# One written order for the first two chunks of an attention and feed-forward kernel, and sign bits put in by ScalarE

## The chip, the cores and the metric

One core of a Trainium2 chip. The metric is the device time of one execution in microseconds (us); lower is better. The engines of the core are TensorE (PE, with its weight loads as PEld), VectorE (DVE), ScalarE (ACT), GpSimd (POOL) and SyncE (SP, which here issues loads).

## The reference

Local attention with global tokens, then a feed-forward layer. Inputs are float32, the two weight matrices float64.

```python
scores = q @ k.T / sqrt(64)                 # 4 batches, 8 heads, 768 rows, head size 64
keep   = (pos_k < n_global) | ((0 <= rel) & (rel < n_local))      # 8 global keys, 96 local ones
dist   = where(global and not local, n_local, abs(rel))
scores = where(keep, scores - 2.0 ** -(head + 1) * dist, -1e9)
a      = exp(scores - max(scores)); a = a / (sum(a) + 1e-9)
x      = (a @ v) as 3072 rows of 512
h      = x @ w_in                                                 # 512 x 2048
out    = (0.5 * h * (1 + erf(h / sqrt(2)))) @ w_out               # 2048 x 512
```

## The kernel before, in words

The 3072 rows are cut into 12 chunks of 256; the 2048 hidden columns into 8 slices of 256. A step (c, s) is chunk c times slice s: a first-layer product into a bank `h` (`m1`, two halves f of 128 columns), Gelu (`gelu`: ScalarE makes `gr`, VectorE its high half `gh` in float16 and the low half `gl`), and a second-layer product into the two halves k of the chunk's output `acc` (`m2`). Each product runs as three float16 products (high x high, high x low, low x high).

Chunks 0 and 1 go through slice after slice together, since the weights are decoded meanwhile; later chunks go through all slices one after the other, with the next chunk's attention between. `STEPS` holds the steps in order: (0,0), three empty places, (0,1), (1,0), (1,1), (0,2), (1,2), (0,3) and so on. From slice 2 on the two chunks share products of 512 columns (L727).

Attention of a chunk goes by pairs of heads: scores into two banks (`scores_pair`), a reduction on VectorE that adds the penalties and finds the largest (L527), exponentials with sums on ScalarE (L561), sums and reciprocals (L570, L573) and scaling (L579) on VectorE, three transposes a head on TensorE (`flip`, L600), copied by ScalarE (L605), products with the values (`av_pair`, L674), and a high half of x by ScalarE (L699, L706) and a low half by VectorE (L211). The scaled probabilities `n` have three buffers.

Weights arrive as float64, four pieces of 512 KB a slice, each as 512 pairs of 32-bit words. A piece is decoded in these parts: the low word is shifted (L249 on GpSimd for slices 0 and 1, L251 on ScalarE for the others); VectorE masks the high word (L257), puts in the sign (L260), joins the low bits (L262); ScalarE makes the high half in float16 (L272) and VectorE the low half (L212 with `winl` or `woutl`). Below, mask, sign and join are the three VectorE parts.

What sets the order: `run` records the work step by step, a scheduler with a timeline of its own puts each engine's instructions in order, and `after` ties single instructions to others. `FILL` and `FILL_T` place products of zeros, `warm_ps`, between the products of the first attention. Each engine then runs its own queue in order, and waits at its head hold up all behind. SyncE's queue issues the loads in order; a load waits when its buffer is taken.

Of the kernel before, what the change touches and what calls it, by code (L numbers as in the profile page):

```python
# [7 lines left out]
F32 = mybir.dt.float32  # L8
# [36 lines left out]
GAP = 3  # L45
STEPS = [(c, s) for s in range(NST) for c in range(2)]
# [40 lines left out]
BLOCKS = (NV - 1, 0, 3, 10, 4, 1, 5, 9, 6, 2, 7, 8)  # L87
WORDS = [T for T in range(33, 90) if T % 2 or T in (62, 70, 78)]
# [26 lines left out]
def slope(h):  # L115
    return 2.0 ** (-(h + 1))


class Fast:
    def __init__(self, tc, ctx, qT, kT, v, w, out, limits):  # L120
# [29 lines left out]
        self.last_unit, self.turns, self.late_rows, self.lows, self.put_off, self.last_max = None, False, [], None, None, None  # L150

    def consts(self):
# [5 lines left out]
        self.scr = const.tile([P, 1], F32, name="scr")  # L158
# [75 lines left out]
    def split_weights(self, s, i):  # L234
        nc = self.nc
        if i == 0:
            if s == LATE:
                self.early.close()
                self.wts = self.ctx.enter_context(self.tc.tile_pool(name="wlate", bufs=1, side="right"))
            if s == NST - 1:  # L240
                self.words.close()
                self.wts = self.ctx.enter_context(self.tc.tile_pool(name="wlast", bufs=1))
            for nm, dst, shape in (("win", self.win, [P, 4, 256]), ("wout", self.wout, [P, 2, 512])):
                dst[s] = tuple(self.wts.tile(shape, F16, name=f"{nm}{k}{s}") for k in "hl")
            self.sw[s] = self.wts.tile([P, 2, 4, 256], F16, name=f"sw{s}")
        w = self.raw.pop((s, i, "w"))
        lw, hw = w[:, :, 0], w[:, :, 1]
        if s < POOLED:
            nc.gpsimd.tensor_scalar(out=lw, in0=lw.bitcast(U32), scalar1=2.0 ** -29, scalar2=None, op0=ALU.mult)  # L249
        else:  # L250
            ins = nc.scalar.activation(out=lw, in_=lw.bitcast(U32), func=AF.Copy, scale=2.0 ** -29).ins  # L251
            if len(self.his) > 1:
                self.after(ins, self.his[-2], "a piece begins when ScalarE is through with the last but one")
            if self.last_table is not None:
                self.after(ins, self.last_table, "a piece comes behind the exponentials of earlier steps")
# [9 lines left out]
    def part_weights(self, s, i):  # L265
        nc = self.nc
        af = self.words_of.pop((s, i)).bitcast(F32)
        if i < 2:
            hi, lo = (x[:, 2 * i:2 * i + 2, :].rearrange("p d f -> p (d f)") for x in self.win[s])
        else:  # L270
            hi, lo = (x[:, i - 2, :] for x in self.wout[s])
# [20 lines left out]
    def load_first(self):  # L292
# [11 lines left out]
        self.raw[0] = (kr, qr)  # L304

# [44 lines left out]
    def load(self, c):  # L350
# [17 lines left out]
        kr = self.nat.tile([P, NP, KW + 96 if cc == 0 else 2 * KW], F32, name=f"kr{c}", tag="kn",  # L368
# [3 lines left out]
        if cc == 0:  # L372
            keys(0, CT, k0)
            keys(CT, 96, k0)
            keys(CT + 96, NG, k0)
# [98 lines left out]
    def scores_pair(self, c, p):  # L474
# [10 lines left out]
        if (c, p) in FILL_S:  # L485
            self.zeros(FILL_S[c, p], sp[0].rearrange("q j k -> q (j k)"))
        prev = self.last_unit if self.turns else self.last_av if EVENTS[c] is not EVF else None
        for j in range(2):
            for a in range(1 if c == 0 and j == 0 else 2):
                for hh in range(2):  # L490
# [3 lines left out]
                    if c == 0 and j == 0:  # L494
                        out, lhs, rhs = sp[hh][:, 0, 0:P], qq[hr, 0:P], kt[hr, 0:P]
                    elif first and j == 0:
                        out, rhs = out[:, 0:P], kt[hr, 0:P]
                    else:
                        if first:
                            rhs = None  # L500
                        elif j == 0:
                            rhs = pairs(kt[hr, :], 96, 96 if a else -96, NC)
                        else:
                            rhs = pairs(kt[hr, :], KW + 192 * a, -96 if a else 96, NC)
                    parts = [(out, rhs)]
                    if c == 0 and j:
                        x = HQ * 3 if a else NG
                        parts = [(out[:, o:o + n], kt[hr, k:k + n]) for o, n, k in ((0, NX, x), (NX, NG, 0), (NX + NG, NC, NC))]
                    for to, keys in parts:
                        ins = nc.tensor.matmul(to, lhsT=lhs, rhs=keys, start=True, stop=True).ins  # L510
                        if prev is not None:
                            self.after(ins, prev, "heads and halves in turn")
                        prev = ins
            if (c, p, j) in FILL:
                prev = self.warm(FILL[c, p, j], prev)
        self.last_unit = prev
        for h in (2 * p, 2 * p + 1) if c == 0 else ():
            ins = nc.vector.tensor_scalar(out=self.pens[:, h, :], in0=self.pen, scalar1=8.0 * slope(h), scalar2=None, op0=ALU.mult).ins
            if self.last_max is not None:
                self.after(ins, self.last_max, "penalties of a pair behind the maxima of the pair ahead")  # L520
# [13 lines left out]

    def zeros(self, n, out):
        prev = self.last_t
        for i in range(n):
            ins = self.nc.tensor.matmul(out, lhsT=self.wz[:, 0:P], rhs=self.wz[:, 0:out.shape[1]],
                                        start=True, stop=True, skip_group_check=True).ins
            self.after(ins, prev, "behind the transposes of the head before")  # L540
            prev = ins
# [51 lines left out]
    def flip(self, c, h):  # L593
# [3 lines left out]
        if (c, h) in FILL_T:  # L597
            self.zeros(FILL_T[c, h], tp.rearrange("k i q -> k (i q)"))
# [8 lines left out]
        if (c, h) == (1, H - 1):  # L607
            scr = nc.scalar.activation(out=self.scr, in_=self.nmax[:, 3 * NP, 0:1], func=AF.Gelu)
            self.after(scr.ins, ins, "behind the last probabilities")
            self.table(scr)  # L610
# [39 lines left out]
    def av_pair(self, c, p):  # L650
# [3 lines left out]
        if p < 2:  # L654
            if c + p == 0:
                self.xs = self.xp.tile([P, 3, NP, 2, CT], F16, name="x")
            self.x[c] = self.xs[:, c % 3]
# [55 lines left out]
    def m1(self, t, f):  # L713
# [16 lines left out]
        prev = self.last_av if (c, s, f) == (0, 1, 1) else self.in_turn if (c, s) in ORDERED and f == 0 else None  # L730
        for d in range(NP):
            for w, e in ((wh, 0), (wh, 1), (wl, 0)):
                ins = nc.tensor.matmul(hp[:, f, :], lhsT=w[:, d, fs], rhs=x[:, d, e, :],  # L733
                                       start=n == 0, stop=n == 3 * NP - 1).ins
                if n == 0 and prev is not None:
                    self.after(ins, prev, "first steps in turn")
                self.turn(ins)
                n += 1
        self.in_turn = ins
# [153 lines left out]
    def m2(self, t, k):  # L893
# [22 lines left out]
        for f in range(2):  # L916
            for g, w in ((gh, wh), (gh, wl), (gl, wh)):
# [3 lines left out]
                if n == 0 and (c, s) in ((0, 1), (1, 0)):  # L921
                    self.after(ins, self.in_turn, "first steps in turn")
                n += 1
        if (c, s) == (0, 1):
            self.in_turn = ins
# [19 lines left out]
    def att(self, T, what, odd=0):  # L945
        for c in range(NCH):
# [37 lines left out]

    def run(self, flag_i):
# [15 lines left out]
        for self.T in range(START[0] - 1, last):  # L1001
# [3 lines left out]
            for (s, i), t in DECODE.items():  # L1005
                if T == t + 1:
                    self.part_weights(s, i)
# [282 lines left out]
```

## Time and profile before

| | |
|---|---|
| median of 3 runs | 610.51 us (610.33 to 613.46) |
| the profiled execution | 609.26 us, of which the span is 607.5 us |
| PE busy | 590.3 us, 97% |
| DVE busy | 480.4 us, 79% |
| ACT busy | 352.1 us, 58% |
| POOL busy | 90.8 us, 15% |

The span goes from the first to the last instruction of the profiled execution. Busy shares are means over stages that have different limits: in the first 60 us TensorE has idle time, later almost none. A matmul's end is modelled, so the row of a matmul can reach into the next one's; the start of the next row tells what a piece costs.

### The profile page before, as it was taken

How to read it: one execution, taken by the hardware profiler on the slowest of the kernel's cores; microseconds unless marked ns; L12 is line 12 of the kernel's file. 1: busy time of each engine (PE TensorE's matmuls, PEld its weight loads, DVE VectorE, ACT ScalarE, POOL GpSimd, SP SyncE). 2: the span in 40 equal slices, each digit the busy share in tenths (PEclk: the TensorE clock that was granted, in tenths of full speed). 3: DMA queues.
4: the chain of work that ended last, by engine and by line, in shares of the span. 5: the costliest groups of instructions: out<-in, count | busy, mean ns of one | idle time of the engine just before them, and what ended most of it. 6: DMA issues, size and time to landing. Idle time of an engine off the chain costs nothing.

```text
span 607.5 us, 18201 instructions
## 1 busy us (share of the span) xinstructions
PE 590.3 (97%) x7377; PEld 456.9 (75%) x7377; DVE 480.4 (79%) x1503; ACT 352.1 (58%) x817; POOL 90.8 (15%) x196
## 2 busy tenths in 40 slices
PE   8889999999999999999999999999999999999996
PEld 6656544445676666888888888888888888888885
DVE  7889999986758964676877877877877877877876
ACT  3577568685647646465566565565565565563332
POOL 3240006222112022021021021021021021020000
PEclk9899999999999999999999999999999999999999
DMA  8948935362521274183194184185284185100001
GB/s 263 254 169 202 335 131 168 100 135 83 138 61 54 89 173 123 38 225 107 55 225 122 40 223 121 67 200 139 83 201 153 64 204 151 66 14 2 36 2 40
DMA packets 105561, 76.74 MB, mean 126 GB/s; under 512 B 53120, under 2 KB 93056, under 8 KB 105472
## 3 DMA queue, kind: packets, MB, share of 16 engines
q1 hardware_dynamic: 102896, 71.85, 42.7%
q10 hardware_dynamic: 2576, 3.67, 1.8%
q8 instruction: 60, 0.98, 0.7%
q14 instruction: 29, 0.24, 0.1%
HBM read 69.21 MB, written 6.29 MB: 124 GB/s over the span
## 4 chain that ended last, share of the span: by engine, by line
PE 81%; DVE 9%; ACT 4%; DMA 3%; issue 1%; POOL 1%; SPq 1%; ACTq 0%; DVEq 0%; POOLq 0%
PE h L733 35%; PE seven L828 24%; PE acc L918 7%; PE av L631 4%; PE s L447 4%; PE acc L903 3%; PE h L727 3%; ACT n L561 2%; DMA w<-w 2%; DVE wb L262 1%; DVE wb L260 1%; DVE n L579 1%; DVE n L527 1%; POOL n L579 1%; SPq L323 1%
## 5 line engine op out<-in xcount | busy, mean ns | idle before, releaser
L733 PE MATMUL h<-x,winh 128*128 128x256 f16 x1344 | 225.2, 273 | 1.1 <-DVE x L211 1.1
L733 PE MATMUL h<-x,winl 128*128 128x256 f16 x672 | 183.1, 273 | 0.0
L733 PEld LDWEIGHTS <-winh 128*128 128x128 f16 x1344 | 130.5, 98 | 21.3 <-issue 1.5
L579 POOL TENSOR_SCALAR n<-n,su 128x160 f32<-128x160 f32 (+1 forms) x160 | 73.0, 474 | 413.6 <-DVE su L573 293.0
L775 ACT ACTIVATE sh<-ss 128x512 f16<-128x512 f32 x64 | 40.3, 630 | 80.5 <-DVE ss L773 80.5
L733 PEld LDWEIGHTS <-winl 128*128 128x128 f16 x672 | 65.7, 98 | 8.2 <-issue 0.7
L768 ACT ACTIVATE gr<-h 128x512 f32<-128x512 f32 x64 | 38.1, 595 | 56.6 <-PE h L733 54.0
L212 DVE SCALAR_TENSOR_TENSOR gl<-gr,gh 128x384 f16<-128x384 f32 (+1 forms) x96 | 57.4, 598 | 10.3 <-ACT gh L889 10.0
L561 ACT ACTIVATE n<-n,mn 128x160 f32<-128x160 f32 x144 | 59.8, 416 | 6.7 <-DVE mn L463 6.0
L773 DVE TENSOR_TENSOR ss<-gr 128x128 f32<-128x128 f32 x128 | 30.9, 281 | 34.6 <-ACT gr L768 34.6
L828 PE MATMUL seven<-sw,sh 128*128 128x256 f16 x384 | 57.4, 273 | 0.0
L828 PEld LDWEIGHTS <-sh 128*128 128x128 f16 x512 | 50.1, 98 | 5.7
L212 DVE SCALAR_TENSOR_TENSOR sl<-ss,sh 128x512 f16<-128x512 f32 x64 | 44.1, 689 | 9.4 <-ACT sh L775 9.2
L828 PEld LDWEIGHTS <-gh 128*128 128x128 f16 x384 | 35.9, 98 | 7.6 <-issue 3.3
L463 DVE CUSTOM_DVE_ANT_0 n<-s,pens 128x160 f32<-128x160 f32 x131 | 35.4, 317 | 5.3 <-PE s L447 5.3
L828 PE MATMUL seven<-sw,sl 128*128 128x256 f16 x192 | 36.6, 273 | 0.1
L774 ACT ACTIVATE gh<-gr 128x384 f16<-128x384 f32 x64 | 33.5, 523 | 2.0
L561 ACT ACT_TABLE_LOAD x22 | 28.2, 1283 | 7.0 <-DMA qr<-qT 6.7
L828 PE MATMUL seven<-wouth,gh 128*128 128x256 f16 x128 | 31.7, 274 | 0.0
L828 PE MATMUL seven<-woutl,gh 128*128 128x256 f16 x128 | 31.5, 273 | 0.0
L211 DVE TENSOR_TENSOR x<-av,x 128x256 f16<-128x256 f32 x41 | 15.3, 414 | 20.5 <-ACT x L644 20.0
L885 ACT ACTIVATE gr<-h 128x512 f32<-128x512 f32 x32 | 19.1, 596 | 20.9 <-PE h L733 16.9
(172 smaller groups left out, 1206.0 us busy)
## 6 DMA issues: line engine op xcount, KB each, us to landing
w<-w SPq DMA_DIRECT2D x32, 512.0 KB, 5.7
c<-w SPq DMA_DIRECT2D x32, 512.0 KB, 4.2
kr<-kT SPq DMA_DIRECT2D x34, 320.0 KB, 4.8
qr<-qT SPq DMA_DIRECT2D x11, 512.0 KB, 4.9
kr<-kT SPq DMA_DIRECT2D x83, 64.0 KB, 4.0
vr<-v SPq DMA_DIRECT2D x24, 176.0 KB, 3.0
out<-o SPq DMA_DIRECT2D x14, 256.0 KB, 2.0
out<-o ACTq DMA_DIRECT2D x8, 256.0 KB, 2.2
```

The costliest lines, as they stand in the source:

```text
L212: return self.nc.vector.scalar_tensor_tensor(out=out, in0=in_, scalar=scale, in1=hi, op0=ALU.mult, op1=ALU.subtract)
L447: ins = nc.tensor.matmul(home[n, u][hh][NG * i:NG * i + NG, :], lhsT=qq[hr, i, o:o + NG], rhs=kt[hr, i, j, k:k + NW], start=not (shared an ...
L463: ins = nc.vector.tensor_tensor_reduce(out=nn[:, 2 * hh + u], in0=home[n, u][hh], in1=pens, scale=-0.125, scalar=3e38, op0=ALU.add, op1=AL ...
L561: self.table(nc.scalar.activation(out=nn, in_=nn, func=AF.Exp, bias=mn[:, i:i + 1], scale=-1.0, accum_out=su[:, i:i + 1]))
L579: ins = eng.tensor_scalar(out=nn, in0=nn, scalar1=su[:, i:i + 1], scalar2=0.0, op0=ALU.mult, op1=ALU.add)
L733: ins = nc.tensor.matmul(hp[:, f, :], lhsT=w[:, d, fs], rhs=x[:, d, e, :], start=n == 0, stop=n == 3 * NP - 1).ins
L768: self.table(nc.scalar.activation(out=gr.rearrange("p i q -> p (i q)"), in_=hp.rearrange("p f q -> p (f q)"), func=AF.Gelu, scale=1.0 / (W ...
L773: self.last_sum = nc.vector.tensor_tensor(out=ss[:, o], in0=x, in1=y, op=op).ins
L774: nc.scalar.activation(out=gh, in_=gr[:, 1:], func=AF.Copy, scale=GS)
L775: self.last_table = nc.scalar.activation(out=sh, in_=ss, func=AF.Copy, scale=GS).ins
L828: ins = nc.tensor.matmul(out, lhsT=g, rhs=w, start=s == 0 and name in ("P1", "P4", "P6", "P3") and i == 0, stop=s >= NST - 4 and i == 2, s ...
L918: ins = nc.tensor.matmul(acc, lhsT=g[:, f, ks], rhs=w[:, f, :], start=s == 0 and n == 0, stop=s == NST - 1 and n == 5).ins
```

## The change

Both chunks' attention, the steps (0,0), (0,1), (1,0), (1,1) and the decoding of slices 0, 1 and 2 no longer go through the loop of `run`. A table, `FRONT`, holds 296 entries, each a letter for a kind of work and figures for chunk, pair or slice and part. `first_steps` records them in the table's order, and `queue` ties each instruction to the last of its engine, so that each engine's order is the table's. Letters that appear below: S scores, R reduction, E exponentials, U sums, N scaling, T transposes, P copy, V values, H and L the halves of x, m and n first and second layer, g Gelu, x and y its halves, w, a, b or s, c, h, l the parts of a weight piece. The loop goes on from step (0,2).

The sign of slice 2's four pieces is put in by ScalarE (`f_sign`, entries s20 to s23) into the upper half of the low word, where the join picks it up; VectorE's sign part stays for slices 0 and 1, and in the loop for later ones.

Chunk 1's keys are loaded once, 352 columns a head pair row, in place of eight loads that laid them out twice; each score product over 192 keys becomes three, over 64, 32 and 96 keys, and the 32 global keys are read from chunk 0's tile. Of the products of zeros, 9 at the start and 6 more stay (`WARM`). A tiny Gelu (`scr`) that loaded Gelu's table early is gone; the first Gelu now comes behind the last exponentials of chunk 1.

```diff
+WARM = {"00": 2, "01": 4}
-FILL = {(0, 0, 1): 4, (0, 1, 1): 9, (0, 2, 1): 4, (0, 3, 1): 4, (1, 0, 1): 4}
-ORDERED = ((1, 0), (1, 1))
-FILL_T = {(1, 6): 6}
-FILL_S = {(1, 1): 0}
+FRONT = ("S00 Q00 W00 R002 R003 E002 R000 R001 E003 Q03 E000 S02 Q02 E001 Q01 U00 N001 S01 N003 N000 R020 w00 N002 "
...
+RESUME = 7
+SCALAR = ()
+SIGNS = ((2, 0), (2, 2), (2, 1), (2, 3))
...
-        kr = self.nat.tile([P, NP, KW + 96 if cc == 0 else 2 * KW], F32, name=f"kr{c}", tag="kn",
+        kr = self.nat.tile([P, NP, CT + NC if c == 1 else 2 * KW], F32, name=f"kr{c}", tag="kn",
                            padded_shape=[P, NP, 4 * KA])
         sync(qr, dap(self.qT, q0, every + [[1, CT]]))
         keys = lambda o, n, k: sync(kr[:, :, o:o + n], dap(self.kT, k, every + [[1, n]]))
-        if cc == 0:
-            keys(0, CT, k0)
-            keys(CT, 96, k0)
-            keys(CT + 96, NG, k0)
+        if c == 1:
+            keys(0, CT + NC, q0 - NC)
...
+    def queue(self, engine, *every):
+        for ins in every:
+            if engine in self.tails:
+                self.after(ins.ins, self.tails[engine], "order of the first steps")
+            self.tails[engine] = ins.ins
+
+    def first_steps(self):
+        for key in FRONT.split():
...
+    def f_scores(self, c, p):
+        kt, qq = (r[:, p] for r in self.raw[c])
+        sp = self.sp[c, p] = [self.bank([P, 2, NK], f"s{c}_{2 * p + hh}") for hh in range(2)]
+        for j in range(2):
+            for a in range(1 if c == 0 and j == 0 else 2):
+                for hh in range(2):
...
+                        x, o = (P + 160 * a, 0) if j else (160 * a, NC + NG)
+                        parts = [(out[:, o:o + NX], kt[hr, x:x + NX]),
+                                 (out[:, NX if j else NC:][:, 0:NG], self.kr0[hr, p, 0:NG]),
+                                 (out[:, NX + NG if j else 0:][:, 0:NC], kt[hr, 192 if j else 64:][:, 0:NC])]
+                    for to, keys in parts:
+                        self.queue("t", self.nc.tensor.matmul(to, lhsT=lhs, rhs=keys, start=True, stop=True))
...
+    def f_sign(self, s, i):
+        w = self.raw[s, i, "w"]
+        hw = w[:, :, 1]
+        if (s, i) in SIGNS:
+            sign = w.rearrange("p f t -> p (f t)").bitcast(F16).rearrange("p (f t) -> p f t", t=4)[:, :, 1]
+            self.queue("a", self.nc.scalar.activation(out=sign, in_=hw, func=AF.Copy, scale=2.0 ** -60))
+        else:
+            a = self.words_of[s, i]
+            self.queue("v", self.nc.vector.scalar_tensor_tensor(out=a, in0=hw, scalar=-0x40000000, in1=a,
+                                                                op0=ALU.bitwise_and, op1=ALU.bitwise_or))
...
-        for self.T in range(START[0] - 1, last):
+        self.xs = self.xp.tile([P, 3, NP, 2, CT], F16, name="x")
+        self.x = {c: self.xs[:, c] for c in range(2)}
+        self.first_steps()
+        for self.T in range(4, last):
```

In the following rows a name like `s1_2` is the tile s of chunk 1, head 2, with a running number behind it; `su0_2` are the sums of pair 2 of chunk 0, and `wb2_3` are the words of piece 3 of slice 2.

SyncE's queue from the queries of chunk 1 to slice 1's words, before:

```order
L323 DMA qr_175<-qT 128x4x256
L323 DMA kr_176<-kT 128x4x160
L323 DMA kr_176<-kT 128x4x64 x2
L323 DMA kr_176<-kT 128x4x160
L323 DMA kr_176<-kT 128x4x32 x4
L323 DMA vr_186<-v 96x512
L323 DMA vr_186<-v 32x512 x2
```

and now:

```order
L330 DMA qr_174<-qT 128x4x256
L330 DMA kr_175<-kT 128x4x352
L330 DMA vr_178<-v 96x512
L330 DMA vr_178<-v 32x512 x2
L330 DMA vr_178<-v 96x512
L330 DMA vr_178<-v 64x2x512 x2
L236 DMA w_0_185<-w 128x1024
```

Eight loads of keys have become one; the values and the words of slice 1 stand behind it as before.

VectorE's queue ahead of the first reduction of chunk 1, before:

```order
L579 TENSOR_SCALAR n0_3_451<-n0_3_451,su0_3_428 128x192
L212 SCALAR_TENSOR_TENSOR winl0_329<-wb0_1_402,winh0_328 128x512
L257 TENSOR_SCALAR wb0_2_469<-w0_2_171 128x512
L260 SCALAR_TENSOR_TENSOR wb0_2_469<-w0_2_171,wb0_2_469 128x512
L527 ISA n1_0_510,nmax_128<-s1_0_496,pens_127 128x192
```

and now:

```order
L1164 ISA wb0_0_352<-w0_0_166,wb0_0_352 128x1024
L1023 TENSOR_SCALAR n0_1_326<-n0_1_326,su0_1_325 128x128
L1023 TENSOR_SCALAR n0_1_326<-n0_1_326,su0_1_325 128x192
L1023 TENSOR_SCALAR n0_2_314<-n0_2_314,su0_2_313 128x128
L1023 TENSOR_SCALAR n0_2_314<-n0_2_314,su0_2_313 128x192
L1148 TENSOR_SCALAR wb0_2_464<-w0_2_170 128x512
L1023 TENSOR_SCALAR n0_2_314<-n0_2_314,su0_2_313 128x192
L1008 ISA n1_0_478,nmax_128<-s1_1_427,pens_127 128x192
```

The reduction now comes ahead of the sums and scalings of chunk 0's last pair, and of most of the decoding of slice 0's pieces 0, 1 and 2.

VectorE's queue around the low half of step (1,1) (`gl6`), before:

```order
L212 SCALAR_TENSOR_TENSOR woutl2_776<-wb2_2_843,wouth2_775 128x512
L257 TENSOR_SCALAR wb3_0_893<-w3_0_209 128x512
L212 SCALAR_TENSOR_TENSOR woutl2_776<-wb2_3_848,wouth2_775 128x512
L257 TENSOR_SCALAR wb3_1_898<-w3_1_211 128x512
L887 TENSOR_SCALAR gh6_984<-gr6_986 128x512
L260 SCALAR_TENSOR_TENSOR wb3_0_893<-w3_0_209,wb3_0_893 128x512
L257 TENSOR_SCALAR wb3_2_950<-w3_2_213 128x512
L260 SCALAR_TENSOR_TENSOR wb3_1_898<-w3_1_211,wb3_1_898 128x512
L212 SCALAR_TENSOR_TENSOR gl6_985<-gr6_986,gh6_984 128x512
```

and now:

```order
L226 SCALAR_TENSOR_TENSOR woutl2_879<-wb2_3_952,wouth2_878 128x512
L1109 TENSOR_SCALAR gh6_993<-gr6_991 128x512
L226 SCALAR_TENSOR_TENSOR woutl2_879<-wb2_2_966,wouth2_878 128x512
L226 SCALAR_TENSOR_TENSOR gl6_994<-gr6_991,gh6_993 128x512
L266 TENSOR_SCALAR wb3_0_1023<-w3_0_201 128x512
L266 TENSOR_SCALAR wb3_1_1028<-w3_1_203 128x512
L266 TENSOR_SCALAR wb3_2_1037<-w3_2_205 128x512
```

Five parts of slice 3's pieces that stood ahead of `gl6` stand behind it now.

## Rows read from the trace of the kernel before

**Rows 1.** Busy time by stretch; then granted clock (1.00 is full), DMA share, GB/s:

```profile
10.00:20.00 10.00, 7.63 (x70) 5.80 (x69) 8.72 (x39) 5.18 (x21) 6.99 (x4) 1.00 1.09 309
...
40.00:50.00 10.00, 8.30 (x94) 5.13 (x92) 8.57 (x30) 8.72 (x27) 0.00 (x0) 1.00 0.22 75
50.00:60.00 10.00, 9.50 (x104) 6.91 (x104) 10.00 (x23) 8.20 (x16) 0.00 (x0) 1.00 1.01 233
...
70.00:80.00 10.00, 10.00 (x48) 4.56 (x47) 10.00 (x20) 5.65 (x10) 0.00 (x0) 1.00 0.87 332
```

**Rows 2.** TensorE's timeline, 60 to 66 us: start, duration, instructions:

```profile
60.91 0.39 PE L918 MATMUL acc<-wouth,gl 128*128 128x512 f16 x1 [0.97 <-DVE gl L212]
...
63.08 0.38 PE L733 MATMUL h<-x,winh 128*128 128x256 f16 x2
...
65.70 0.38 PE L918 MATMUL acc<-wouth,gh 128*128 128x512 f16 x1
```

**Rows 3.** VectorE's timeline, 66 to 70 us:

```profile
66.26 0.42 DVE L257 TENSOR_SCALAR wb<-w 128x512 int32<-128x512 int32 x1
...
67.87 0.68 DVE L260 SCALAR_TENSOR_TENSOR wb<-w,wb 128x512 int32<-128x512 int32 x1
68.47 0.41 DVE L257 TENSOR_SCALAR wb<-w 128x512 int32<-128x512 int32 x1
68.81 0.68 DVE L260 SCALAR_TENSOR_TENSOR wb<-w,wb 128x512 int32<-128x512 int32 x1
69.41 0.68 DVE L212 SCALAR_TENSOR_TENSOR gl<-gr,gh 128x512 f16<-128x512 f32 x1
```

**Rows 4.** VectorE's waits to 75 us; then its groups, 28.5 to 70.1:

```profile
DVE su L570 <- ACT n L561: 5.3, 6, 1.4
...
L570 DVE TENSOR_SCALAR su<-su 128x4 f32<-128x4 f32 x4 | 1.1, 275 | 2.3 <-ACT n L561 2.3
```

**Rows 5.** ScalarE's groups, 20 to 75 us:

```profile
L251 ACT ACTIVATE w<-w 128x512 int32<-128x512 uint32 x10 | 6.2, 671 | 0.0
```

**Rows 6.** VectorE's timeline at the first reductions of chunk 1:

```profile
28.56 0.35 DVE L527 CUSTOM_DVE_ANT_0 n<-s,pens 128x192 f32<-128x192 f32 x1
...
28.83 0.35 DVE L527 CUSTOM_DVE_ANT_0 n<-s,pens 128x192 f32<-128x192 f32 x1
```

**Rows 7.** SyncE's timeline; then loads issued 8:10 and 10:10.6, with landing:

```profile
8.76 0.43 SPq L323 DMA_DIRECT2D qr<-qT  x1
10.37 10.33 SPq L323 DMA_DIRECT2D kr<-kT  x8
...
qr<-qT SPq DMA_DIRECT2D x1, 512.0 KB, 8.7
...
kr<-kT SPq DMA_DIRECT2D x1, 320.0 KB, 8.1
```

**Rows 8.** TensorE's timeline: scores and transposes, two records a float32 product:

```profile
8.51 1.54 PE L510 MATMUL s<-kr,qr 64*128 64x128 f32 x28 [0.46 <-DMA kr<-kT]
...
17.74 0.82 PE L600 MATMUL t<-ident,n 128*128 128x128 f32 x6
...
27.11 0.97 PE L510 MATMUL s<-kr,qr 64*64 64x192 f32 x16
```

**Rows 9.** Busy time by stretch, with the granted clock behind POOL's:

```profile
18.60:20.20 1.60, 0.00 (x0) 0.00 (x0) 1.29 (x7) 1.60 (x7) 0.00 (x0) 1.00 1.11 221
22.20:25.50 3.30, 3.30 (x24) 2.41 (x21) 2.21 (x11) 1.94 (x10) 0.00 (x0) 0.50 0.64 184
```

**Rows 10.** VectorE's timeline, beside GpSimd and without; then GpSimd's group to 75 us:

```profile
32.27 1.51 DVE L579 TENSOR_SCALAR n<-n,su 128x192 f32<-128x192 f32 x4
...
34.04 1.13 DVE L212 SCALAR_TENSOR_TENSOR woutl<-wb,wouth 128x512 f16<-128x512 f32 x1
...
39.12 1.01 DVE L579 TENSOR_SCALAR n<-n,su 128x192 f32<-128x192 f32 x4
...
L249 POOL TENSOR_SCALAR w<-w 128x512 int32<-128x512 uint32 x8 | 13.9, 1733 | 20.9 <-DMA w<-w 20.2 <-DVE n L579 0.4
```

More of the change, by code (lines that the diff above doesn't have):

```diff
@@ L242, in split_weights @@
                 self.wts = self.ctx.enter_context(self.tc.tile_pool(name="wlast", bufs=1))
-            for nm, dst, shape in (("win", self.win, [P, 4, 256]), ("wout", self.wout, [P, 2, 512])):
-                dst[s] = tuple(self.wts.tile(shape, F16, name=f"{nm}{k}{s}") for k in "hl")
-            self.sw[s] = self.wts.tile([P, 2, 4, 256], F16, name=f"sw{s}")
+            self.new_weights(s)
         w = self.raw.pop((s, i, "w"))
         lw, hw = w[:, :, 0], w[:, :, 1]
[L248 to L255, printed above, removed]
+        ins = nc.scalar.activation(out=lw, in_=lw.bitcast(U32), func=AF.Copy, scale=2.0 ** -29).ins
+        if len(self.his) > 1:
+            self.after(ins, self.his[-2], "a piece begins when ScalarE is through with the last but one")
+        if self.last_table is not None:
+            self.after(ins, self.last_table, "a piece comes behind the exponentials of earlier steps")
         a = self.sm.tile([P, 512], I32, name=f"wb{s}_{i}", tag="o", bufs=3)
@@ L267, in part_weights @@
         af = self.words_of.pop((s, i)).bitcast(F32)
[L268 to L271, printed above, removed]
+        hi, lo = self.halves(s, i)
         ins = nc.scalar.activation(out=hi, in_=af, func=AF.Copy, scale=WS).ins
@@ L493, in scores_pair @@
                     out, lhs = sp[hh][a * HQ:(a + 1) * HQ, j, :], qq[hr, o:o + HQ]
[L494 to L497, printed above, removed]
-                    else:
[L499 to L515, printed above, removed]
+                    if j == 0:
+                        keys = pairs(kt[hr, :], 96, 96 if a else -96, NC)
+                    else:
+                        keys = pairs(kt[hr, :], KW + 192 * a, -96 if a else 96, NC)
+                    ins = nc.tensor.matmul(out, lhsT=lhs, rhs=keys, start=True, stop=True).ins
+                    if prev is not None:
+                        self.after(ins, prev, "heads and halves in turn")
+                    prev = ins
         self.last_unit = prev
[L517 to L520, printed above, removed]
         ns = self.pp.tile([P, 2, 2 * NK], F32, name=f"n{c}_{p}", tag="n")
@@ L533, in scores_pair @@
             self.pt_n[c, 2 * p + hh] = nn
[L535 to L541, printed above, removed]
     def warm(self, n, prev=None):
@@ L606, in flip @@
         self.pt_t[c, h] = pt
[L607 to L610, printed above, removed]
     def av_windows(self, c, part):
@@ L945, in att @@
     def att(self, T, what, odd=0):
-        for c in range(NCH):
+        for c in range(2, NCH):
             r = T - START[c]
@@ L1036, in run @@
                 self.gelu(T + 1)
+            if T < RESUME:
+                continue
             self.att(T, "pt", 1)
```

203 lines of the change are left out of this document (180 added, 23 removed), and 13 rows, old and new, of the table FRONT.

## The prediction

> **What bounds the kernel now.** I read the table of stretches first, then VectorE's timeline, TensorE's, the waits, and last the loads. From 70 us on TensorE is busy 10.0 of 10 us in nearly every stretch, and what it does there is the same work in nearly the same order in both programs; so the change is worth what it takes off the front, the part up to the last second-layer product of the first four steps. In the front TensorE waits (7.63 and 8.30 of 10 us, filler products included), while VectorE goes from 8.7 of 10 to 10.0 by 50 us [rows 1]. VectorE sets the pace: at 60.91 TensorE has its last long wait of the front, 0.97 us for a low half that VectorE makes [rows 2].
>
> Where does the front end? VectorE ends its last piece of it, the low half of step (1,1), at 70.01 (start 69.41, and such pieces follow each other every 0.60). Between 66.26 and there stand five pieces that belong to slice 3, not to the front; from start to next start the three masks take 0.34 each and the two sign pieces 0.60, 2.21 in all (one of each mask shown) [rows 3]. So VectorE's front is worth 67.8 us. TensorE has, from 60.91 on and without a pause, 34 products of 512 columns (10 of them last from 60.91 to 63.08, so 0.217 each) and 24 of 256 (63.08 to 65.70, 2.62) [rows 2]: 60.91 + 7.37 + 2.62 = 70.9. It ends 3.1 us behind VectorE.
>
> **What the change does to that.** In the new table VectorE's last piece is again the low half of (1,1). TensorE starts its last 36 second-layer products when the low half of (0,1) is there, 4.3 us of VectorE's table earlier (six pieces of 0.60, two of 0.335); it can pass only four of them before the last words of slice 1 come 0.6 later, so 32 x 0.217 = 6.9 stand behind that, 7.5 - 4.3 = 3.2 us after VectorE. The lag is the old one. What VectorE's table gains, the kernel gains.
>
> Removed from VectorE: four sign pieces. One lasts 0.68, but back to back they cost 0.60 each [rows 3], so 2.4 us. ScalarE gets them; none of its rows is this form, and the nearest is its own piece on the words, 671 ns [rows 5]; it is busy 8 to 9 of 10 us between 40 and 60 and less around them [rows 1], and the early Gelu with its two table loads leaves it, so four times 0.6 cost nothing there. If ScalarE were late, high halves of slice 2 would be, and their price is at most those 2.4 us back.
>
> Removed too: VectorE's waits for exponentials, 5.3 us in six [rows 4]. The first, until the sums at 9.73, is given by the first four exponentials and mostly stays; scaled penalties of two more pairs fill 0.8 of it. The others go if the table always has something else ready.
>
> Added: one wait that I can place. VectorE's first reduction of chunk 1 (28.56 now [rows 6]) stands in the table much earlier. Summing VectorE's new order from the first sums at 9.73, which stay (twelve reductions of 0.25, 3.0, since half of them are narrower than the 0.27 of [rows 6]; three pairs of sums with their reciprocals, an estimated 1.3 from the 0.275 of a sum [rows 4]; twelve scalings of 0.24, 2.9 [rows 10]; three masks, one sign, one join of words, 2.2 [rows 3]; an estimated 1.7 for what GpSimd's pieces stretch meanwhile, from [rows 10]), it gets there at about 20.8. The scores are not there. The keys of chunk 1 are one load of 704 KB instead of eight, behind the queries, which land 8.7 us after 8.76; the first 320 KB of keys land 8.1 after 10.37, 1.0 us later [rows 7]. So 704 KB take 2.2 and land at 19.6; I take 19.5. Then TensorE does the scores of pair 1, transposes of pair 1 of chunk 0, the scores of pair 0, and transposes again (VectorE writes into a buffer that these still read). What 24 products of a pair cost no row shows: 8 products with as many columns take 0.97, and 14 products that are mostly of these pieces 1.54, so by count 2.6 [rows 8]. I take 1.8, nearer the second, because its groups overlap the next by their drain. With transposes at 0.40 a head [rows 8] the reduction can start at 19.5 + 1.8 + 0.35 + 1.8 + 0.45 = 23.9; the ends are 22.2 and 25.5.
>
> The clock makes this later. TensorE idles in the table from about 14.7 to 19.5. Before, an idle stretch from 18.6 to 20.2 was followed by the lower level (1.2 GHz) from 22.2 to 25.5, and then by the full one [rows 9]. At half speed for 3.4 us it loses at most 1.7; I take 0.8, half: 24.7.
>
> From there VectorE's work is what it did before from 28.56 to 70.01, 41.45, less slice 3 (2.21), less its idle time of 2.26 (the two waits of 0.87 and 1.39; [rows 4] has 2.3), that is 36.98; less the signs, 2.4; plus what the old order had done by 28.56 and the new has not: five word pieces of 0.60 (3.0), two low halves of x (0.67), one sums pair and four scalings (1.36), 5.0. Together 39.6. Idle time in it: between 0 and the old 2.26; the table puts several pieces between the last exponential and its sum, so I take 0.6. End: 24.7 + 39.6 + 0.6 = 64.9 against 67.8, a gain of 2.9 us.
>
> Behind the front nothing is added: slice 3's words need 6.1 us of VectorE (four masks, eight pieces of 0.60), the next two steps of TensorE 3.2 + 5.2. POOL's four pieces of slice 1 come earlier, at about 26 to 33 instead of 29.75 to 37.2, since the loads ahead are shorter; there four scalings took 1.51 against 1.01 later without POOL, and a low half 1.13 against 0.68 [rows 10]. The same number of pieces meets the same kind of work; I change nothing.
>
> The Trainium skill (SBUF — State Buffer, section Who interferes with whom) says of that meeting that VectorE and GpSimd take a shared port pair for a whole instruction and the other is blocked until it ends. The rows agree in direction: what is stretched are scalings and pieces with two operands in SBUF. They do not agree in size: a piece of POOL's lasts 1.73 us, and four scalings together lose 0.5 [rows 10]. By the page's rule in full this would be a rival of its own, below.
>
> **Sum.** The profiled execution took 609.26 us (607.5 of span); the median of the runs is 610.51, 1.25 more. 609.26 - 2.9 = 606.4, and on the scale of the median 607.6. A measurement of this kernel can tell about 0.5%, 3.05 us, from no change: the forecast lies at that edge.
>
> **Rivals.**
> - The gain is given back in waits along VectorE's table. For: every engine is now tied in order, and VectorE waits for a low half of x behind product, copy and cast of two other engines; the 0.6 may be 3. Against: before it had the same chains and only 2.3. Time: 606.4 + 2.4 = 608.8, on the median's scale 610.
> - The table runs as if without the wait: scores at 0.97 a pair, no low clock. Then the reduction starts at 22.2, with no idle time the end is 61.8, a gain of 6.0: 604.5. For: the columns are those of the old products. Against: short products repeat a fixed share in the 14-product row.
> - Slower, by TensorE's clock: filler products fall from 40 in all to 15, and in the first 40 us TensorE's work waits in short pieces. If the lower level lasts 15 us after 19.5 instead of 3.4, TensorE loses 7.5 where 0.8 is counted, and VectorE waits for scores and values: +6.7 - 2.9 = 3.8, 614.3. It decides from some 13.5 us of low clock on (2.9 + 3.05 + 0.8 = 6.75 at half a microsecond each). For: the one low stretch of before came with fillers in place. Against: it lasted 3.4 us although TensorE did only small products in it [rows 9].
> - Slower, by GpSimd blocking VectorE: four pieces of slice 1 that hold VectorE up by a whole 1.7 each, 6.8 where the rows have about 0.9: 5.9 - 2.9 = 3.0, 613.5. The traces speak against it, with losses of 0.1 to 0.5 per piece [rows 10]; it is what the page's rule would give.
>
> That the change doesn't do what it says I leave out: each engine's order stands in the built program.
>
> **Chances.** Forecast 0.52, with a range of its own from 605.3 to 609.5; gain given back 0.21; no wait 0.15; clock 0.09; GpSimd 0.03. About half of the forecast's case lies below 607.46 (610.51 - 3.05): faster 0.27 + 0.15 = 0.42; same 0.25 + 0.21 = 0.46; slower 0.12. For the range I go from 603.8, below the no-wait case, to 611.6, above the given-back case; the slower cases lie outside.
>
> **What would show it.** First reduction of chunk 1 at 24.7 (22.2 to 26), with TensorE's scores as what ended VectorE's wait of about 4 us; the keys' landing at 19.5; a low clock of some 3.4 us around 19 to 23; VectorE's last piece of step (1,1) at 64.9; from there on TensorE 10 of 10. Wrong if VectorE idles more than 2 us after its first reduction of chunk 1, if the front ends at 61 or before, or if time goes away or comes behind 75 us.

## The result and the profile after

The changed kernel takes 616.35 us in the median of 7 runs (615.89 to 618.47), the kernel before 610.33 us in 7 runs beside it: a ratio of 1.010, with a 95% interval from 1.0076 to 1.0123. It is slower by 6.0 us where 2.9 us less were forecast, and it lies outside the range. The profiled execution took 615.89 us (span 614.1), 6.6 more than that of before.

The table of stretches of the changed kernel, to be set against [rows 1] (same columns: busy time of TensorE, its weight loads, VectorE, ScalarE, GpSimd, then granted clock, DMA share, GB/s):

```profile
10.00:20.00 10.00, 5.16 (x73) 3.84 (x68) 9.55 (x45) 5.86 (x24) 6.56 (x4) 0.91 1.06 326
20.00:30.00 10.00, 8.47 (x112) 7.06 (x114) 1.43 (x9) 2.42 (x8) 3.07 (x2) 0.50 0.94 280
...
50.00:60.00 10.00, 9.09 (x98) 6.01 (x97) 9.69 (x23) 7.10 (x12) 0.00 (x0) 1.00 0.47 165
60.00:70.00 10.00, 6.07 (x29) 2.90 (x28) 8.82 (x17) 7.08 (x12) 0.00 (x0) 0.83 1.11 307
70.00:80.00 10.00, 10.00 (x48) 4.50 (x47) 9.78 (x19) 4.56 (x9) 0.00 (x0) 1.00 1.04 314
```

One row stands out: from 20 to 30 us VectorE, which sets the pace of the front, is busy 1.43 of 10 us, and TensorE has half its clock. VectorE's timeline shows one wait there:

```profile
20.08 0.31 DVE L1023 TENSOR_SCALAR n<-n,su 128x192 f32<-128x192 f32 x1
28.97 0.36 DVE L1008 CUSTOM_DVE_ANT_0 n<-s,pens 128x192 f32<-128x192 f32 x1 [8.57 <-PE t L1029]
```

The first reduction of chunk 1 starts at 28.97; it stood at 28.56 before [rows 6], with much more done ahead of it. What it waits for is on TensorE (scores, transposes, scores, transposes; the last row is a pair's scores at full clock):

```profile
14.42 1.17 PE L988 MATMUL warm_ps<-wz 128*128 128x512 f32 x4
21.53 2.89 PE L984 MATMUL s<-kr,qr 64*64 64x64 f32 x48 [5.95 <-DMA kr<-kT]
24.35 0.90 PE L1029 MATMUL t<-ident,n 128*128 128x128 f32 x3
25.18 2.92 PE L984 MATMUL s<-kr,qr 64*64 64x64 f32 x48
28.03 0.90 PE L1029 MATMUL t<-ident,n 128*128 128x128 f32 x3
...
33.92 1.76 PE L984 MATMUL s<-kr,qr 64*64 64x64 f32 x48
```

TensorE waits 5.95 us for the keys, and then every piece takes longer than the same piece does at 33.92. The next rows show the clock there: busy time by stretch, with the granted clock behind GpSimd's, to be set against [rows 9]:

```profile
15.60:18.20 2.60, 0.00 (x0) 0.00 (x0) 2.46 (x13) 1.89 (x8) 2.14 (x2) 1.00 1.07 352
18.20:21.50 3.30, 0.00 (x0) 0.00 (x1) 2.19 (x8) 0.00 (x0) 0.00 (x0) 0.51 1.10 251
21.50:31.90 10.40, 10.37 (x124) 8.61 (x124) 2.63 (x12) 3.66 (x12) 4.81 (x4) 0.50 0.74 237
31.90:34.00 2.10, 2.06 (x35) 1.50 (x35) 1.91 (x8) 1.86 (x7) 1.44 (x1) 1.00 0.01 4
```

TensorE does nothing from 15.6 on, the clock falls to the lower level (1.2 GHz) at 18.2, and it stays there to 31.9, through 10.4 us in which TensorE is busy with small float32 products. In the kernel before it came back after 3.4 us.

Later VectorE ends its last piece of the front, and TensorE pauses once more (VectorE's and TensorE's timelines, to be set against [rows 3] and [rows 2]):

```profile
70.10 0.43 DVE L1109 TENSOR_SCALAR gh<-gr 128x512 f16<-128x512 f32 x1 [0.90 <-PE acc L1123]
70.45 0.69 DVE L226 SCALAR_TENSOR_TENSOR woutl<-wb,wouth 128x512 f16<-128x512 f32 x1
71.05 0.68 DVE L226 SCALAR_TENSOR_TENSOR gl<-gr,gh 128x512 f16<-128x512 f32 x1
```

```profile
64.86 0.39 PE L1123 MATMUL acc<-wouth,gh 128*128 128x512 f16 x1 [3.00 <-DVE gh L1109]
...
66.39 0.61 PE L1123 MATMUL acc<-wouth,gl 128*128 128x512 f16 x1 [0.93 <-DVE gl L226]
...
77.38 0.38 PE L1123 MATMUL acc<-wouth,gl 128*128 128x512 f16 x1
```

VectorE's front ends at 71.65 (start 71.05 and 0.60), against 67.8 before. TensorE's ends at 77.60, and from 72.64 on 2.37 us of it are shared products of step (0,2): 75.2, against 70.9 before. So the front is 4.3 us longer. From some 165 us on each Gelu stands 6.1 us later than in the kernel before: another 1.8 come behind the front.

### The profile page after: what moved, and what is told of

The parts are those of the page before. It is cut to its first block, busy times and chain, and to the rows that moved or that the text cites. A ratio compares the mean times of both kernels' runs of the same rounds, so it can differ in the third digit from the quotient of the medians.

```text
span 614.1 us, 18375 instructions
## 1 busy us (share of the span) xinstructions
PE 590.7 (96%) x7480; PEld 457.5 (74%) x7480; DVE 478.4 (78%) x1499; ACT 354.7 (58%) x818; POOL 87.0 (14%) x196
## 4 chain that ended last, share of the span: by engine, by line
PE 80%; DVE 10%; ACT 4%; DMA 4%; issue 1%; SPq 0%; ACTq 0%; DVEq 0%
PE h L701 33%; PE seven L793 24%; PE acc L883 7%; PE av L602 4%; PE s L452 4%; PE h L696 2%; DMA w<-w 2%; DMA kr<-kT 2%; PE acc L868 2%; PE acc L1123 1%; ACT n L538 1%; PE s L984 1%; DVE gl L226 1%; DVE winl L226 1%; DVE wb L269 1%
## 5 line engine op out<-in xcount | busy, mean ns | idle before, releaser
L701 PE MATMUL h<-x,winh 128*128 128x256 f16 x1280 | 214.2, 273 | 0.8 <-DVE x L225 0.8
L701 PE MATMUL h<-x,winl 128*128 128x256 f16 x640 | 174.4, 273 | 0.0
L701 PEld LDWEIGHTS <-winh 128*128 128x128 f16 x1280 | 124.6, 98 | 19.6 <-issue 0.8
L556 POOL TENSOR_SCALAR n<-n,su 128x160 f32<-128x160 f32 (+1 forms) x160 | 70.2, 459 | 425.4 <-DVE su L550 288.5
L733 ACT ACTIVATE gr<-h 128x512 f32<-128x512 f32 x64 | 38.1, 596 | 56.3 <-PE h L701 53.9
L701 PEld LDWEIGHTS <-winl 128*128 128x128 f16 x640 | 62.6, 98 | 7.3
L602 PE MATMUL av<-ptb,vr 32*64 32x128 f32 (+4 forms) x1392 | 30.2, 265 | 0.1
L602 PEld LDWEIGHTS av<-ptb,vr 32*64 32x64 f32 x1392 | 26.0, 131 | 5.4 <-issue 4.2
```

The lines of the kernel that those rows point to most:

```text
L556: ins = eng.tensor_scalar(out=nn, in0=nn, scalar1=su[:, i:i + 1], scalar2=0.0, op0=ALU.mult, op1=ALU.add)
L602: ins = nc.tensor.matmul(banks[i][hh * D:(hh + 1) * D, u0 * NG:u1 * NG], lhsT=vv[rows, b, hh * D:(hh + 1) * D], rhs=g, start=n == 0 and no ...
L733: self.table(nc.scalar.activation(out=gr.rearrange("p i q -> p (i q)"), in_=hp.rearrange("p f q -> p (f q)"), func=AF.Gelu, scale=1.0 / (W ...
```

## The experiments

Each is run beside the kernel before (median 610.0 to 610.9 in the four sets). Where an edit adds a line, a line number in a profile row is one or more higher than in the changed kernel.

**The clock alone: `e1_warm`.** Products of zeros fill TensorE's pause ahead of chunk 1's scores.

```diff
-WARM = {"00": 2, "01": 4}
+WARM = {"00": 2, "01": 32}
```

> The changed kernel with 32 products of zeros instead of 4 between the transposes of head 3 and the first scores of chunk 1, so that TensorE is busy from 14.4 to about 21.4 us, when the keys land. Theory A (the clock: TensorE's pause from 15.6 to 21.5 lets the granted clock fall to 0.5 from 18.3 to 31.6, and scores of 2.9 us a pair and transposes of 0.9 us at that level make the first reduction of chunk 1 late): no low stretch, scores 1.8 a pair and transposes 0.45, the first reduction at 25.9 to 26.2 instead of 28.97, and the execution 3 us or more shorter, 613 or less on the scale of the median of 616.35. Theory B (the wait for the keys itself, the clock is only seen beside it): the first reduction no earlier than 28.3, 615.5 to 617.

Measured: 615.94 us (4 runs, 615.18 to 617.78), not to be told from the changed kernel. Yet scores take 1.78 and 1.80 us a pair and transposes 0.55, and the first reduction starts at 26.91, though the keys landed at 22.27 in this execution, 0.9 later. Each theory holds in one half only: the clock does delay the reduction, and the gain is lost again. The stretches around the second pause show where some of it may go:

```profile
55.00:63.80 8.80, 4.98 (x34) 3.03 (x32) 8.32 (x17) 6.68 (x10) 0.00 (x0) 1.00 1.03 307
63.80:70.60 6.80, 5.87 (x15) 2.09 (x15) 5.45 (x11) 2.85 (x5) 0.00 (x0) 0.50 1.08 292
70.60:75.00 4.40, 4.40 (x21) 1.96 (x20) 4.30 (x9) 0.99 (x2) 0.00 (x0) 1.00 1.04 219
```

TensorE is busy 4.98 of 8.8 us ahead of 63.8, and then its products at the end of the front run at the lower level for 6.8 us, where the changed kernel has 3.4. This execution is the slowest of the four (617.78) and has one more low stretch, from 125 to 128.6 us. The run `e10_warm_end` below fills the second pause as well.

**The keys alone: `e2_keys`.** Queries and keys of chunk 1 go ahead of two pieces of slice 0's words.

```diff
-        for i in range(4):
+        for i in range(2):
             self.load_weights(0, i)
         self.load(1)
+        self.after(self.last_load, self.last_word, "keys behind two pieces of words")
+        self.last_word = self.last_load
+        for i in range(2, 4):
+            self.load_weights(0, i)
         self.load_v(1)
```

> The changed kernel with the queries and keys of chunk 1 loaded ahead of the third and fourth piece of slice 0's words. The keys land two pieces of 512 KB earlier, 2.6 us (a piece per 1.3), at about 18.8 instead of 21.4. Theory B (lateness of the keys): the first reduction at about 26.4, the execution 2.5 us shorter, 613.8. Theory A (clock): TensorE still pauses for 3 us from 15.6, the clock still falls at about 18.3, the scores still take 2.9 a pair; the first reduction comes 2.6 earlier as well, but the low stretch stays as long as the work in it is short, 10 us or more, and the execution gains at most 2.5. The two together differ in the next run.

Measured: 613.10 us (10 runs, 610.70 to 615.08). The keys land at 17.57, 3.8 earlier; in the profiled run TensorE pauses 2.09 and the clock does not fall there. The first reduction starts at 22.21, 6.8 earlier, and the Gelu of step (1,1) 5.5 earlier. The ten runs spread over 4.4 us, in line with their mean clock: those at 0.995 or 0.996 took 610.7 to 610.8, those at 0.979 to 0.983 took 613.5 to 615.1. So with the shorter pause the clock is lost in some runs and not in others; at which place the slow ones lost it is not shown, since the profiled run is one of the fast ones.

**Both: `e3_both`.** The edit of `e2_keys`, and 20 products of zeros.

> Both: queries and keys of chunk 1 ahead of two pieces of words, and 20 products of zeros instead of 4 behind the transposes of head 3 (14.4 to 18.8 us). Theories A and B add up: first reduction at 23.3 to 23.7, near the 23.9 that the prediction had without its clock loss; the execution 5.5 us shorter than the changed kernel's, 610 to 611, about the time of the kernel before. If the time then stays above 613, the loss is elsewhere: in VectorE's table behind the first reduction or in the signs on ScalarE.

Measured: 613.99 us (7 runs), where 610 to 611 was expected. The expected reduction time holds (23.52), but this is 1.3 later than in the run before, since the zeros last to 18.98 while the keys are there at 17.49. Fillers that outlast the wait they fill cost time themselves. The second pause is not filled here (granted clock 0.50 from 62.3 to 65.6 us); what the rest of the miss is was not separated.

**The second pause alone: `e6_end`.** The changed kernel with 13 products of zeros ahead of step (0,1)'s second-layer product.

```diff
-WARM = {"00": 2, "01": 4}
+WARM = {"00": 2, "01": 4, "11": 13}
... (from here on parts of lines of FRONT)
-l13 a22 c22 n010 h22
+l13 a22 c22 W11 n010 h22
...
+            out = self.acc[0, 0] if c else self.warm_ps
...
```

> The changed kernel with 13 products of zeros (added into chunk 0's output bank, so nothing is computed otherwise) ahead of the second-layer product of step (0,1), where TensorE pauses from 61.9 to 64.9 us for a high half that VectorE makes, and 0.9 more for the low half; from 66.0 the clock is then at 0.5 for 3.4 us, while TensorE starts on the front's last products. Theory D (this second pause and the low stretch behind it cost time that nothing hides): no low stretch at 66, the later steps 1 to 1.7 us earlier, 614.7 to 615.3 where the changed kernel has 616.35. Theory E (VectorE sets the end of the front, TensorE's clock there is hidden): the later steps at the same times within 0.5, 616 to 616.7.

Measured: 617.31 us (5 runs). The clock stays at 1.00 from 32.6 us on, and steps from 145 us on start within 0.04 us of the changed kernel's: theory E (the medians, 1.0 apart, lie within the spread of these five runs). The stretch from 66 us in the changed kernel and in `e6_end`, and VectorE's last piece of the front in `e6_end`:

```profile
66.00:69.40 3.40, 3.01 (x8) 1.08 (x9) 3.17 (x6) 1.76 (x4) 0.00 (x0) 0.50 1.10 287
66.00:69.40 3.40, 2.95 (x13) 1.28 (x14) 3.37 (x7) 1.76 (x4) 0.00 (x0) 1.00 1.14 294
...
70.18 0.68 DVE L226 SCALAR_TENSOR_TENSOR gl<-gr,gh 128x512 f16<-128x512 f32 x1
```

In the changed kernel this second low stretch (3.4 us, from 66.0) costs time at the end of the front and none at the end: without it VectorE's last piece starts 0.9 earlier (70.18 against 71.05, the wait of 0.90 at 70.10 is gone), TensorE's front, counted as above, ends at 74.0 instead of 75.2, and between 75 and 130 us TensorE waits 2.5 us for VectorE's halves instead of 0.8.

**Both pauses, late keys: `e10_warm_end`.** 32 and 13 products of zeros.

> The changed kernel with late keys as they are, but with both pauses of TensorE filled (32 products of zeros ahead of chunk 1's scores, 13 at the end of the front). The second kernel with filled pauses and early keys took 610.3. If the clock behind the first pause is the larger part of the loss: the first reduction 4.6 us behind the keys' landing and not 7.6, no stretch at the lower level before 600 us, the execution near 613. If lateness of the keys is the larger part: 615 or more.

Measured: 613.65 us (7 runs, 612.82 to 614.07), 2.7 less than the changed kernel. The profiled execution has no low stretch before 600 us. The keys land at 21.87, the first reduction starts 4.64 later; in the changed kernel it is 7.58 (28.97 - 21.39). So the lower clock costs 2.9 us at this place, and 2.5 (Gelus from 165 us on) to 2.7 (medians) of them reach the end. The stretch of the scores, and TensorE's and VectorE's timelines:

```profile
22.20:27.00 4.80, 4.80 (x112) 4.05 (x110) 0.49 (x3) 1.88 (x6) 0.00 (x0) 1.00 1.04 303
```

```profile
22.00 1.77 PE L984 MATMUL s<-kr,qr 64*64 64x64 f32 x48
23.71 0.55 PE L1030 MATMUL t<-ident,n 128*128 128x128 f32 x3
24.19 1.81 PE L984 MATMUL s<-kr,qr 64*64 64x64 f32 x48
25.92 0.55 PE L1030 MATMUL t<-ident,n 128*128 128x128 f32 x3
```

```profile
26.51 0.36 DVE L1009 CUSTOM_DVE_ANT_0 n<-s,pens 128x192 f32<-128x192 f32 x1 [5.82 <-PE t L1030]
```

**Both pauses, early keys: `e7_keys_end`.** 12 and 13 products of zeros, and the edit of `e2_keys`.

> The early keys of the second run (two pieces of words behind them), 12 products of zeros instead of 4 ahead of chunk 1's scores (to about 17.2, just short of the keys' landing at 17.5) and the 13 at the end of the front. Each run of the second kernel lay between 610.7 and 615.1, with a mean clock from 0.996 down to 0.979. Theory D: with both pauses filled the mean clock is 0.999 in most runs, the runs lie closer together, and the median falls from 613.1 to 609 to 611, the time of the kernel before. Theory E: 612.5 to 613.5, and the spread stays.

Measured: 610.33 us (11 runs, 609.76 to 610.86; mean clock 0.998 to 1.000), against 610.32 of the kernel before: the same. Theory D holds here, with a spread of 1.1 us instead of 4.4. Against the run before this one, keys that land 4.3 us earlier (17.56 against 21.87) are worth 3.3 us.

**The order behind the front: `e11_order`.** The last kernel, and ScalarE's cast of slice 0's weight sums is tied behind chunk 2's first Gelu and its high half.

```diff
-        nc.scalar.copy(hi, t)
+        self.cast = nc.scalar.copy(hi, t).ins
...
                 self.gelu(T + 1)
+                if T == 18:
+                    self.after(self.cast, self.last_table, "behind chunk 2's first gelu")
```

> The kernel with early keys and both pauses filled (610.3), and one cast of ScalarE (sums of slice 0's second-layer weights, which waits 3 us for VectorE at 147 to 150 us) placed behind chunk 2's first Gelu and its high half. Theory F (behind the front the old scheduler's order holds up TensorE where it did not in the kernel before: 1.05 us at 153.6 for a high half of ScalarE, whose Gelu stands behind that cast and an output copy): TensorE does not wait there, steps from 155 us on are 1.0 us earlier, 609.3. Otherwise the wait moves to the next place that needs VectorE, and it stays 610.3.

Measured: 608.66 us (12 runs, 607.87 to 609.44), ratio to the kernel before 0.9974, interval 0.9958 to 0.9991: a quarter of a per cent less than the kernel before, and 1.7 us less than `e7_keys_end`. Theory F holds. TensorE in the kernel with early keys and filled pauses, at the place (it is the changed kernel's wait at 159.06, of 1.06):

```profile
152.04 0.38 PE L701 MATMUL h<-x,winh 128*128 128x256 f16 x2
152.25 0.27 PE L701 MATMUL h<-x,winl 128*128 128x256 f16 x1
153.58 0.39 PE L883 MATMUL acc<-wouth,gh 128*128 128x512 f16 x1 [1.05 <-ACT gh L854]
```

and with the cast behind the Gelu:

```profile
151.47 0.38 PE L701 MATMUL h<-x,winh 128*128 128x256 f16 x2
151.68 0.27 PE L701 MATMUL h<-x,winl 128*128 128x256 f16 x1
151.79 0.38 PE L883 MATMUL acc<-wouth,gh 128*128 128x512 f16 x1
```

The wait is gone, and the steps behind are 2.1 us earlier in the profiled runs, 1.7 in the medians, more than the 1.05 expected: 0.6 of it is already there at 152, ahead of the edit, from a shorter wait for x at an earlier step.

**The signs back on VectorE: `e5_signs`** (the changed kernel) **and `e13_signs_back`** (the kernel of `e11_order`).

```diff
-SIGNS = ((2, 0), (2, 2), (2, 1), (2, 3))
+SIGNS = ()
...
... (parts of lines of FRONT)
-U12 h10 N120 s20 N121 l10
+U12 h10 N120 N121 l10
...
-V13 a20 y00
+V13 a20 s20 y00
```

The entries s21, s22 and s23 move in the same way, each behind its a.

> The changed kernel with slice 2's four signs back on VectorE, each right behind its mask. If moving them was worth the 2.4 us of the prediction: 618.7. Theory C (ScalarE's sign takes 1.1 us a piece and not 0.6, sits between copies and Gelu, and holds up the joins, so that nothing was gained): 616.4, no change, or shorter.

> The best kernel so far (early keys, both pauses filled, ScalarE's cast behind chunk 2's first Gelu: 608.7) with slice 2's four signs back on VectorE, each behind its mask; the clock is at full level here, so it doesn't blur the term as it did in the run with the changed kernel's late keys (620.5 against 616.4). The prediction's term: four pieces of 0.60 on VectorE that the front's end follows one for one, 611.1, and the Gelu of step (1,1) 2.4 us later. If it is much less (under 609.5), VectorE did not set the front's end. If more (612 or above), the old scheduler's order behind the front has changed with it, and the 2.4 is read from the Gelu of step (1,1).

Measured: 620.54 us (4 runs), 4.2 more than the changed kernel, and 609.99 us (11 runs), 1.3 more than `e11_order`, where 2.4 more was expected. The second is read without a change of clock. There the Gelu of step (1,1), on ScalarE's timeline of `e11_order` and of `e13_signs_back`:

```profile
63.02 0.58 ACT L1100 ACTIVATE gr<-h 128x512 f32<-128x512 f32 x1
```

```profile
65.75 0.58 ACT L1100 ACTIVATE gr<-h 128x512 f32<-128x512 f32 x1
```

2.73 later: the term of 2.4 is about right at the front's end, while 1.7 are left behind 140 us; behind the front the loop's order differs between the two programs. Theory C falls, although ScalarE's piece is even longer than it says (group of the changed kernel, 20 to 75 us; two in a row took 2.50 in `e8_before_sign`):

```profile
L1156 ACT ACTIVATE w<-w 128x512 f16<-128x512 int32 x4 | 5.4, 1350 | 0.1
```

**The signs alone, without the table: `e8_before_sign` and `e9_before_signs`**, the kernel before with its old scheduler; `SIGNS` is (2,) in the first and (2, 3, 4) in the second.

```diff
...
-        nc.vector.scalar_tensor_tensor(out=a, in0=hw, scalar=-0x40000000, in1=a,
-                                       op0=ALU.bitwise_and, op1=ALU.bitwise_or)
+        if s in SIGNS:
+            sign = w.rearrange("p f t -> p (f t)").bitcast(F16).rearrange("p (f t) -> p f t", t=4)[:, :, 1]
+            self.after(nc.scalar.activation(out=sign, in_=hw, func=AF.Copy, scale=2.0 ** -60).ins, ins_w, "sign behind the shift")
+        else:
+            nc.vector.scalar_tensor_tensor(out=a, in0=hw, scalar=-0x40000000, in1=a,
+                                           op0=ALU.bitwise_and, op1=ALU.bitwise_or)
```

> The kernel before with slice 2's four signs on ScalarE, each behind its shift, everything else by the old scheduler. If VectorE sets the front's end there too: 2.4 us of VectorE go and 607.5 to 609 is left of 610.4. The other way: ScalarE's sign lasts 1.1 us net and stands ahead of Gelu and high halves in its queue, the joins wait for it, and the time is 610.4 or more.

> The same with the signs of slices 2, 3 and 4 on ScalarE. VectorE is busy 10.0 of 10 us up to 90 us in the kernel before, so 4.8 us more go from it there; but TensorE has only 0.9 us of pause between 60 and 90. If the front alone counts: as the run before, within 0.5 us. If TensorE's pauses of 2 us between 90 and 130 come from VectorE's backlog: 1 to 2 us shorter than the run before.

Measured: 618.46 us (5 runs) and 617.06 us (5 runs), against 610.32. Slower by 8.1 and 6.7, and the second 1.4 less than the first. The waits of the first from 20 to 150 us (engine and line, releaser: us in total, times, longest):

```profile
DVE gh L893 <- ACT gr L891: 4.7, 3, 3.4
DVE gh L893 <- PE acc L909: 3.6, 1, 3.6
...
PE h L733 <- ACT gr L891: 3.6, 1, 3.6
```

VectorE and TensorE now wait for Gelu. The old scheduler places all four engines' work anew once one piece moves, so these runs tell what this edit does to that program, not what four pieces on ScalarE cost by themselves: whether the pieces' length or the new order makes Gelu late was not separated. The profiled run of the first also has two low stretches of TensorE's clock, around 22 to 29 and 134 to 138 us.

**Later signs: `e12_late`.** The kernel of `e7_keys_end`, with slices 3 and 4 signed by ScalarE in the loop (the edit just shown, for those slices).

> The kernel with early keys and both pauses filled (610.3), and the signs of slices 3 and 4 on ScalarE too, in the loop behind the table. VectorE is busy 9 to 10 of 10 us from 60 to 130 us; 8 pieces of 0.6 us go from it, and TensorE's waits for VectorE between 88 and 130 (2.6 us: 1.3 for a low half, 1.1 for x, 0.2 for a high half) can fall by that: 608 to 609.5. Other way: ScalarE's 8 more pieces of 1.1 us stand ahead of Gelu as they did in the kernel before with signs on ScalarE (617 to 618), and it takes 611 or more.

Measured: 613.17 us (10 runs), 2.8 more than `e7_keys_end`: the second of the two outcomes. TensorE again waits for Gelu (2.5 us at one place), with the same limit on what this shows.

```profile
PE h L701 <- ACT gr L855: 2.5, 1, 2.5
```

## Why the prediction was wrong

Term by term, in the profiled executions: the first reduction of chunk 1 starts at 28.97 where 24.7 was forecast, 4.3 later (1.9 from the keys, 2.1 from the clock, 0.2 from scores and transposes); from there to VectorE's last piece of the front it takes 42.7 in place of 40.2, 2.5 more; TensorE ends 3.6 behind VectorE in place of 3.1; and 1.8 come behind the front, where nothing was forecast. Together that is 9 us, the distance from 2.9 less to 6.1 more.

The experiments take the time back in other portions, in medians: the changed kernel 616.35; the clock kept up 613.65 (2.7 less); early keys 610.33 (3.3); the order behind the front 608.66 (1.7). These 7.7 us are not the forecast's errors one by one: the first takes away all that the low clock cost, of which the forecast had counted 0.8, and the early keys land at 17.6, 1.9 ahead of the 19.5 of the forecast.

- *"704 KB take 2.2 and land at 19.6"*: failed. The keys landed at 21.39, 3.4 behind the queries (18.00). The changed kernel's load of the keys, issued at 10.31, and the last two key pieces of the kernel before, issued at 19.3 and 20.0 (KB each, median us to landing):

```profile
kr<-kT SPq DMA_DIRECT2D x1, 704.0 KB, 11.1
```

```profile
kr<-kT SPq DMA_DIRECT2D x2, 64.0 KB, 3.3
```

  The forecast took the distance between the queries' landing and that of the first key piece [rows 7] for that piece's duration. The trace of before had the better number: all eight pieces, 1152 KB, landed by 23.09, 5.7 us behind the queries at 17.41, that is 4.9 us per 1000 KB, and by it 704 KB take 3.5 and land at 20.9 by the forecast's landing of the queries. The error of the forecast is 1.9 us here; no run has the keys at 19.5.
- *"At half speed for 3.4 us it loses at most 1.7; I take 0.8"*: failed. The low stretch lasted 13.7 us, and cost 2.9 where 0.8 was counted. The rival "slower, by TensorE's clock", with a chance of 0.09, had this mechanism and a low stretch of 15 us, but put 7.5 us on it; that its 614.3 lies near the measured 616.35 is in part luck. The argument against it, that in [rows 9] the clock came back after 3.4 us with only small products, did not carry over to a pause of 5.95 us in place of 1.6.
- *The scores*: 24 products at 1.8 a pair and transposes of 0.35 to 0.45 were right at full clock (1.78 and about 0.48 from start to start). The first reduction is 4.6 us behind the keys there, 4.4 in the forecast without its clock loss.
- *VectorE from the first reduction to its last piece*: 39.6 and 0.6 of idle were forecast, 42.7 measured (28.97 to 71.65). The work was right and the 0.6 failed: VectorE is busy 39.7 us of it and idle 3.0.

```profile
28.97:71.65 42.68, 36.93 (x420) 25.94 (x421) 39.72 (x117) 32.95 (x79) 4.21 (x3) 0.93 0.50 148
```

  The first rival named this (chance 0.21: "the 0.6 may be 3"). Its longer waits alone are 1.8 us (0.9 at 70.10, which `e6_end` shows to come from the second low stretch, and two under 0.5). In `e11_order` the same way is 43.1 (22.12 to 65.18), with no wait over 0.46 behind the first piece, but with scalings of 400 ns where the changed kernel's take 311, 20 of each, and 8.2 us of GpSimd's pieces beside them in place of 4.2. That this kernel's front ends at 65.2, as forecast (64.9), is two errors against each other: an earlier start and a longer way.
- *"The lag is the old one", 3.2 us*: nearly right, 3.6, with a second low stretch in it; in `e6_end`, without that stretch, it is 3.2.
- *"So the change is worth what it takes off the front"*: only in part. `e6_end` ends the front 1.3 us earlier on TensorE than the changed kernel and is level with it from 145 us on, and in `e13_signs_back` 2.7 at the front's end become 1.7. Behind the front VectorE is as full as TensorE: 10.00 of 10 us each from 70 to 80 us in the kernel before [rows 1].
- *"Removed from VectorE: four sign pieces", 2.4*: right in size at the front (2.7 at the Gelu of step (1,1)). ScalarE's 0.60 a piece was wrong, 1.35, and cost nothing that could be seen in this table.
- *"Behind the front nothing is added"*: failed, by 1.8 us. Shown of it is one wait: TensorE waits 1.06 us at 159.06, at chunk 2's first Gelu, where it did not before, and `e11_order` takes that wait away. That the order behind the front was nearly the same did not help: an output copy stood on the other side of one Gelu. The wait is not the whole account: on the way there the kernel before has waits of 2.0 us at two other places (100.27 and 122.38), the changed kernel 2.2 in all. The rest of the 1.8 was not separated.
- *GpSimd blocking VectorE by a whole piece*: not seen; the scalings of `e11_order` just named are 0.09 us longer in the mean.

## What to carry to other kernels

When a table moves a consumer ahead, its load has to move too, and the engine that feeds it needs work in the gap: here TensorE's clock turned VectorE's wait of 5.8 us into one of 8.6. Take a transfer's duration from a whole group of like transfers, from the landing ahead of it to its last landing, and not from the first piece of it alone. After a change in one stage, look at the first places where the next stage switches engines: here one cast on the other side of a Gelu was worth a wait of 1.05 us, and 1.7 in the medians.

## What the runs showed of the hardware

- The granted clock of TensorE stayed at 0.50 from 18.2 to 31.9 us, though TensorE was busy 10.37 us of the last 10.40 of it. It had done nothing from 15.6 to 21.5. With the pause filled by products of zeros (`e10_warm_end`) the same work ran at 1.00.
- In the kernel before the time goes with the mean clock too: over the 24 runs beside `e11_order` the mean clock is 0.989 to 1.000 and the time 612.8 to 607.8. The seven at 0.998 or more have a median of 609.1, so at an equal clock the best kernel here (608.66) is little better than the one before.
- While the keys were carried, the DMA engines were as busy as otherwise (share 1.10) and moved 251 GB/s, against 352 just ahead of them (rows of 15.60 and 18.20 above). Why was not tried.
